# Four scheduling edits in an attention and Strassen-expert kernel: a pause in operand preparation, a load moved to SyncE, operands fetched two pieces ahead, and x sums queued together

## The chip, the cores and the metric

The kernel runs on one core of a Trainium2 chip. The metric is the device time of one execution in microseconds (us). Before the change three runs took 1164.88, 1165.45 and 1167.73 us; the median is 1165.45.

The core has five engines that this text names: PE (TensorE, matmuls; its weight loads are PEld), DVE (VectorE), ACT (ScalarE), POOL (GpSimd) and SP (SyncE, which here only issues DMAs). Each works through its own instructions in order and waits on semaphores for the others.

## What is computed

```python
# lightning attention, blocks of 64, (B, H, S, D) = (4, 8, 768, 64)
intra = einsum(q_b, k_b) * Dmask;  intra = intra @ v_b
inter = (q_b * lam_pow) @ kv_state;  out_b = intra + inter
kv_state = lam_block * kv_state + (k_b * rev_pow).T @ v_b
x = out.transpose(0, 2, 1, 3).reshape(3072, 512)
# four experts, F = 1024
p = probs / (probs.sum(-1) + 1e-9)
out = sum over e of p[:, e:e+1] * (relu(x @ w1[e]) @ w2[e])
```

All of it is in float32.

## The kernel before

**Groups and units.** The 3072 tokens are three groups of 1024. A unit is one expert on one group; there are twelve. While PE computes the second product (hidden times w2) of one unit, it computes the first product (x times w1) of the next one, interleaved: each unit has seven steps (`i`), one for each of Strassen's seven products, and each step eight slots (`x`) that alternate between second and first product (L1659 and on). Unit 0 begins at about 92 us. Before it lie the attention of group 0 and the first product of unit 0, written out as a list of calls (L1580 to 1590); the attention of the other groups is put into slots of later units.

**Plain and nested units.** Both products use Strassen's scheme. The first product (L1047) uses it twice, one level inside the other. The second product is plain, with one level, in the first five units (`second_product`, L1101), and nested from unit 5 on (`nested_product`, L1400; `NEST = 2 * E - 3`, L140). The first nested unit begins at about 600 us. A nested product needs gated hidden blocks (`gated`, L875: POOL multiplies by the gate, `m<-m,decay`), their sums (`outer_sums`, L888: ACT copies a block to a PSUM bank, `hp`, and DVE subtracts into `hT`; `inner_sums`, L918: POOL, `acc<-...`), and operands made of w2.

**Preparation.** The sums of the blocks of w1 and w2 that Strassen's products need are made by POOL ahead of time, stored in DRAM (`w1_ops`, `w2_ops`, `w2_sums`, all named w_ops or w_sums in the profile) and loaded back when they are due. These pieces of work are `chores` (for w2: `prepare_w2_ops`, L335; tiles `w2b`, `w2o`, `ops`). `pump` (L202), called after every slot, begins the next chore when a small model of POOL's and the DMA queues' load says so (`begins`, L208). `until` forces chores on when something is needed that isn't made yet. The stores go through a queue of their own and are issued by SP.

**Loads.** `send` (L109; the issue is L114) issues a DMA on SP unless told otherwise. `feed3` (L1139) loads an operand of a nested second product into tiles `w2t`, from a pool of six buffers (L75). Each of the seven pieces of a unit takes four tiles (`k` = 0 to 3; the last is half as large). Two are loaded at the begin of a step, and two behind slots 1 and 3 (L1681 and a few lines on); before the first nested unit two are loaded, so that the loads run two tiles ahead. `ws_in` are the operands of the first product, `xs` the x blocks and their sums. Results of group 1's plain unit are stored as `partial`, finished blocks as `parked`. The order in which SP issues all this is the order in which the program is written.

**Probabilities.** `load_probs` (L1570) loads the experts' probabilities (24 x 128 rows of 4 floats) into a part of the `decay` tile, issued by ACT. DVE makes the gates of it at about 72 us. A DMA's issue waits until the DMA before it that uses the same one of eight semaphores has landed; the semaphores are dealt out in turn over all issues of SP and ACT in the order of the built program.

**x sums.** The first product of unit 1 needs four subtractions (`x_steps`, L392) of each of seven x tiles. `own_x` (L1433) puts those of a tile into `own_sums`; the slots take them from there, one at a time, when DVE's modelled load allows it, and `first_product` (L1023) takes what is left when it needs them.

Of the kernel before, what the change touches and what calls it, by code (L numbers as in the profile page):

```python
# [21 lines left out]
def kernel(  # L22
# [30 lines left out]
    nc = tc.nc  # L53
# [4 lines left out]
    P = nc.NUM_PARTITIONS  # L58
# [42 lines left out]
    def packet(ap):  # L101
        n, step = 1, 1
        for stride, size in reversed(ap.ap[1:]):
            if stride != step or size == 1 and stride != 1:
                break
            n, step = n * size, step * size
        return n

    def send(out, in_, by=None):  # L109
        n = 4 * min(packet(out), packet(in_))  # L110
        moved[0] = max(moved[0], now[0]) + 4 * math.prod(out.shape) / n * (9 + n / 25) / 16 / 1714
        if by is None:
            asked[0] = max(asked[0], now[0]) + 0.27
        (by or nc.sync).dma_start(out=out, in_=in_)  # L114
# [13 lines left out]
    now, busy, free, filled, moved, asked, spare = [0], [0.0], [0.0], [0.0], [0.0], [0.0], []  # L128
# [11 lines left out]
    NEST = 2 * E - 3  # L140
# [46 lines left out]


    chores, queue, late, results, made = [], [], [], [], set()
    LEFT, packed = 1, []  # L190
    FULL = 4

    def store(f):
# [8 lines left out]
    def pump(pace=1.0, force=False):  # L202
        all_added(None if force else now[0])
        while results:
            results.pop(0)()
        while late and (force or late[0][0] <= now[0]):
            late.pop(0)[1]()
        begins = chores and (  # L208
            force or free[0] <= now[0] and max(moved[0], asked[0]) < now[0] + FULL
            and not (packed and busy[0] > now[0] + 1)  # L210
        )
        while queue and (force or queue[0][0] <= now[0] or begins and len(queue) > LEFT):
            queue.pop(0)[1]()
        if begins:
            begin = free[0] = max(free[0], now[0] - 1)
            was = max(busy[0], now[0])
            chores.pop(0)()
            free[0] = max(free[0], begin + max(pace * (busy[0] - was), (5 if len(chores) > 13 else 7) if spare else 1))
# [298 lines left out]
    for r in range(2):  # L517
        for ac in range(NHP):
            h = 4 * r + ac
            nc.vector.tensor_tensor_scan(  # L520
                out=s_decay[:, r, ac], data0=lam_bc[:, h:h + 1].to_broadcast([P, BL]), data1=blk_ident,
# [10 lines left out]
    for ac in range(NHP):  # L532
        nc.vector.tensor_tensor_scan(
            out=q_decay[:, ac], data0=lam_q[:, ac:ac + 1].to_broadcast([P, BL]), data1=zeros[:, 0:BL],
# [15 lines left out]
    probs = decay[:, 6, 0:96].rearrange("p (t e) -> p t e", e=E)  # L550
# [391 lines left out]
    SEQ = ("M1", "M5", "M6", "M2", "M7", "M3", "M4")  # L942
# [490 lines left out]
    def own_x(m, g=0, wait=0):  # L1433

        steps = to_do[m] = []

        def sub(f):
            def step():
                steps.pop()
                f()  # L1440
                if not steps:
                    made.add(("x", g, m))

            steps.append(step)

        for f in x_steps(g, m, nc.vector):
            sub(f)
        own_sums.extend(after(wait, f) for f in steps)
# [119 lines left out]
        chores.extend((*prepare_w2(0), *(raw[n] for n in ("A11", "A22", "A21"))))  # L1568

    def load_probs():  # L1570
        nc.scalar.dma_start(out=probs, in_=moe_domain_probs.rearrange("(t p) e -> p t e", p=P))

    def loads(*of):
        return lambda: [raw_w1(0, x) if isinstance(x, str) else load(x) for x in of]
# [84 lines left out]
    for at, (g, e) in enumerate(units):  # L1659
        if at == 0:  # L1660
            chores.extend(prepare_w2(2) + prepare_w1(3) + prepare_w2(3))
            chores.extend(prepare_w2_ops(2, False) + prepare_w1(0))
            for x in (3, 0):
                chores.extend(prepare_w2_ops(x, True))
        ahead = units[at + 1] if at + 1 < len(units) else None
        nested, nests = at >= NEST, ahead and at + 1 >= NEST
        if at == NEST:
            until(("w1", 0, "M4"))
            chores.extend(prepare_w2_ops(1, True))
            spare.append(True)  # L1670
        if at == NEST - 1:
            forget()
            packed.append(True)
        blocks, banks = {}, {}
        for i in range(7):
            if fill2:
                feed2(*fill2.pop(0))
            if not nested:
                later_operands(g, e, SEQ2[i])
            if nested or (nests and i == 6):  # L1680
                for _ in range(2 if ahead else 16 if i == 0 else 4 if i > 1 else 0):  # L1681
                    if fill3:
                        feed3(*fill3.pop(0))
            if nests and i == 2:
                nc.scalar.dma_start(
                    out=gate_bc, in_=gate_rows[ahead[0] - 1, :, ahead[1]].partition_broadcast(P),
                )
            if nested:
                pair = (at * 7 + i) % 2 if ahead else i % 3
                b = nested_product(at, SEQ3[i], (("q01", "q02"), ("q11", "q12"), ("g1", "g3"))[pair])  # L1690
                if i < 6 and (at, SEQ3[i + 1]) != PLAIN:
                    inner_sums(at, SEQ3[i + 1])
            else:
                b = second_product(g, e, SEQ2[i], banks)
            if nests and i == 6:
                inner_sums(at + 1, SEQ3[0], nested)
                if at + 1 == EARLY[0]:
                    inner_sums(*EARLY, True)
            a = []
            if ahead:  # L1700
                a = first_product(*ahead, SEQ[i], blocks, ("g1", "g3"))
            if nested and (at, SEQ3[i]) == END:
                b[6:6] = [lambda: (give("M4", 1, ("s0", "s1"), (1,)), turn_end(1, "q11"))]
                b[5:5] = [lambda: (give("M4", 0, ("s0", "s1"), (1,)), turn_end(0, "q12"))]
            if not ahead:
                order = [[], b[0:2], [], b[2:4], [], b[4:6], [], b[6:]]
            elif nested:
                order = [b[0:2], a[0:2], b[2:4], a[2:4], b[4:6], a[4:6], b[6:8], a[6:8]]
            else:
                order = [b[0:1], a[0:2], b[1:2], a[2:4], b[2:3], a[4:6], b[3:5], a[6:8]]  # L1710
            turned_back = list(after_last.get(SEQ3[i], ())) if nested and not ahead else []
            if at == 0 and i < 6:
                own_x(SEQ[i + 1])
            for x, part in enumerate(order):
                for f in part:
                    if f:
                        f()
                now[0] += 1
                if (at - 2 * E + 1, i, x) in first_steps:
                    first_steps.pop((at - 2 * E + 1, i, x))()  # L1720
                if joins:
                    joined()
                elif (ahead or x % 2 == 0 and x + i) and not (nests and i == 6 and x == 7):
                    if nested or nests:
                        rest()
                    else:
                        took = False
                        for of in (lately, background, own_sums):
                            if of and (not took or fits() or of is background and len(of) > 1):
                                take(of)  # L1730
                                took = True
                if nested or nests:
                    take(aside)
                    if own_sums and fits():
                        take(own_sums)
                if ending and fits():
                    end_first()
                if nested and ahead and x in (1, 3) and fill3:
                    feed3(*fill3.pop(0))
                if turned_back and x > 0:  # L1740
                    for y in turned_back.pop(0):
                        if SEQ3[i] == END[1]:
                            give(*y[:2], ("s0", "s1"), *y[2:])
                        else:
                            give_across(*y)
                if fill and at * 7 + i >= 6 and x in ((0, 1) if at * 7 + i < 13 else (1, 3, 5) if at * 7 + i == 13 else FEED[nested]):
                    feed(*fill.pop(0))
                while steps and (at * 7 + i) * 8 + x == steps[0][0]:
                    steps.pop(0)[1]()
                if at == 0 or x % 2:  # L1750
                    trickle(1, nc.scalar if at == 0 and x % 2 else None)
                for h in range(1, NG):
                    if x == 3 and 0 <= at * 7 + i - FILL[h] < 7:
                        x_fill(h, SEQ[at * 7 + i - FILL[h]])
                pump(PACE[g])
# [30 lines left out]
```

## Time and profile before

| | |
|---|---|
| median of three runs | 1165.45 us |
| the profiled execution | 1169.61 us |
| its span, first to last instruction | 1167.8 us |
| PE busy | 1148.6 us (98%) |
| PEld busy | 993.3 us (85%) |
| DVE busy | 824.5 us (71%) |
| POOL busy | 796.9 us (68%) |
| ACT busy | 317.1 us (27%) |
| DMA packets | 309258, 269.21 MB, mean 231 GB/s |
| mean granted TensorE clock | 0.995 |

Times in the profile are counted from the span's start. A timeline line gives start, duration, engine, source line, operation, what it writes and reads (`out<-in`), the number of merged instructions, and in brackets the idle time before it with what ended it. Lines of the waits give total, times and longest. L117 is the helper that issues every tensor_tensor, L114 the one that issues most DMAs, so those are told apart by their tiles. Names lose their numbers: `m` are all blocks of the hidden layer, `pg`, `pM`, `pq` and `q` are PSUM banks of the products. A float32 matmul is recorded as two instructions.

### The profile page before, as it was taken

Reading aid. Unit: us, or ns where it says so; the run is one execution under the profiler, and the core shown is the slowest. Engines: PE = TensorE matmul, PEld = TensorE weight load, DVE = VectorE, ACT = ScalarE, POOL = GpSimd, SP = SyncE. Lnnn points to the kernel's source line nnn. Section 1 sums busy time; section 2 is a strip of 40 time slices with the busy share of each in tenths; the row PEclk is TensorE's granted clock in tenths of the full one; section 3 lists DMA queues with packets and bytes.
Section 4 is the critical chain, followed back from the end, with each engine's and each line's share of the span. In section 5 each row is a group of like instructions: output and inputs, shape, how many; then the busy total and the mean of one; then the engine's idle time right before and its main releaser. Section 6 shows DMA issues by size and latency. Waiting matters only on the chain.

```text
span 1167.8 us, 21962 instructions
## 1 busy us (share of the span) xinstructions
PE 1148.6 (98%) x8011; PEld 993.3 (85%) x8011; DVE 824.5 (71%) x1516; ACT 317.1 (27%) x638; POOL 796.9 (68%) x752
## 2 busy tenths in 40 slices
PE   8899999999999999999999999999999999999998
PEld 7788888888888888888878888888888888888887
DVE  4485786578478857946765677998875677777785
ACT  4312122112201211221233342232243342341231
POOL 2836417746742984774796798896897793793894
PEclk9899999999999999999999999999999999999999
DMA  9894667999899999796867678966767866657542
GB/s 195 198 280 125 182 196 216 298 290 292 263 313 306 286 301 304 231 350 201 276 189 231 198 217 256 328 206 195 222 224 254 236 179 201 176 177 207 158 189 72
DMA packets 309258, 269.21 MB, mean 231 GB/s; under 512 B 141536, under 2 KB 244128, under 8 KB 309152
## 3 DMA queue, kind: packets, MB, share of 16 engines
q1 hardware_dynamic: 287744, 262.48, 73.6%
q10 hardware_dynamic: 21408, 5.33, 2.3%
q8 instruction: 64, 1.05, 0.4%
q14 instruction: 42, 0.34, 0.1%
HBM read 194.83 MB, written 77.10 MB: 233 GB/s over the span
## 4 chain that ended last, share of the span: by engine, by line
PE 85%; POOL 6%; DVE 4%; DMA 3%; issue 1%; SPq 1%; ACT 0%; ACTq 0%; POOLq 0%; DVEq 0%
PE pg L1047 35%; PE pq L1400 21%; PE q L1101 18%; POOL acc L117 3%; PE pM L1502 2%; DVE m L117 2%; PE pc L1502 2%; POOL m L117 2%; PE op L748 1%; PE sp L694 1%; DMA w2t<-w_ops 1%; PE op L766 1%; SPq L114 1%; PE sp L701 1%; DVE sums L117 1%
## 5 line engine op out<-in xcount | busy, mean ns | idle before, releaser
L1047 PE MATMUL pg<-xs,ws_in 128*128 128x256 f32 x1960 | 473.3, 381 | 4.9 <-DVE m L117 4.7
L1047 PEld LDWEIGHTS pg<-xs,ws_in 128*128 128x128 f32 x1960 | 368.5, 190 | 60.7 <-DVE m L117 10.7
L117 DVE TENSOR_TENSOR m<-pg,m 128x512 f32<-128x512 f32 x451 | 307.8, 688 | 122.4 <-PE pg L1047 105.4
L1101 PE MATMUL q<-w2t,m 128*128 128x256 f32 x1120 | 264.6, 379 | 0.0
L1101 PEld LDWEIGHTS q<-w2t,m 128*128 128x128 f32 x1120 | 212.7, 190 | 29.0
L117 POOL TENSOR_TENSOR m<-m,decay 128x512 f32<-128x512 f32 x112 | 143.4, 1299 | 83.6 <-ACT m L1059 75.5
L1400 PE MATMUL pq<-acc,w2t 128*128 128x256 f32 x688 | 170.5, 381 | 1.5 <-DMA w2t<-w_ops 1.4
L117 DVE TENSOR_TENSOR sums<-pq,sums 128x256 f32<-128x256 f32 x272 | 113.1, 421 | 71.9 <-PE pq L1400 64.4
L1400 PEld LDWEIGHTS pq<-acc,w2t 128*128 128x128 f32 x688 | 130.9, 191 | 20.8 <-issue 2.3
L1059 ACT ACTIVATE m<-m 128x512 f32<-128x512 f32 x132 | 83.1, 632 | 197.7 <-DVE m L117 191.4
L117 DVE TENSOR_TENSOR m<-m,m 128x512 f32<-128x512 f32 x112 | 97.1, 867 | 3.5 <-ACT m L1059 3.5
L1055 ACT COPY m<-pg 128x512 f32<-128x512 f32 x88 | 51.6, 587 | 147.1 <-PE pg L1047 137.3
L1119 DVE SCALAR_TENSOR_TENSOR acc<-q,gate,acc 128x256 f32<-128x256 f32 x108 | 51.9, 480 | 51.0 <-PE q L1101 50.5
L117 POOL TENSOR_TENSOR acc<-hT,hT 128x512 f32<-128x512 f32 x56 | 71.0, 1284 | 14.1 <-PE pq L1400 14.1
L117 POOL TENSOR_TENSOR acc<-hT,acc 128x512 f32<-128x512 f32 x56 | 71.4, 1275 | 6.4 <-PE pq L1400 1.8
L1400 PE MATMUL pq<-hT,w2t 128*128 128x256 f32 x288 | 74.0, 379 | 0.1
L979 ACT COPY up<-m 128x512 f32<-128x512 f32 x56 | 32.5, 590 | 127.5 <-DVE m L117 127.3
L117 POOL TENSOR_TENSOR w2o<-w2b 128x512 f32<-128x512 f32 x26 | 34.4, 1347 | 42.6 <-DMA w2b<-in_moe_w_dram 30.0
L1400 PEld LDWEIGHTS pq<-hT,w2t 128*128 128x128 f32 x288 | 54.6, 190 | 7.9 <-DVE sums L117 0.5
L899 ACT COPY hp<-m 128x512 f32<-128x512 f32 x84 | 48.5, 590 | 43.8 <-POOL m L117 22.2
L1400 PE MATMUL pq<-m,w2t 128*128 128x256 f32 x228 | 59.4, 384 | 0.1
L117 POOL TENSOR_TENSOR xs<-xs 128x256 f32<-128x256 f32 x28 | 23.8, 849 | 42.5 <-DMA xs<-x_blocks 40.9
(140 smaller groups left out, 1365.3 us busy)
## 6 DMA issues: line engine op xcount, KB each, us to landing
w2t<-w_ops SPq DMA_DIRECT2D x129, 256.0 KB, 4.0
ws_in<-w_ops SPq DMA_DIRECT2D x40, 512.0 KB, 5.2
ws_in<-w_ops SPq DMA_DIRECT2D x60, 256.0 KB, 3.6
ws_in<-w_ops SPq DMA_DIRECT2D x40, 384.0 KB, 3.7
w2b<-in_moe_w_dram SPq DMA_DIRECT2D x56, 256.0 KB, 5.1
w_ops<-ops SPq DMA_DIRECT2D x28, 512.0 KB, 4.8
w2t<-w_sums SPq DMA_DIRECT2D x40, 256.0 KB, 4.5
w_sums<-w2o SPq DMA_DIRECT2D x16, 512.0 KB, 5.0
```

What stands on the lines that cost most here:

```text
L114: (by or nc.sync).dma_start(out=out, in_=in_)
L117: eng.tensor_tensor(out=o, in0=a, in1=b, op=op)
L694: nc.tensor.matmul(out=sp[r][half[x], ac * BL:(ac + 1) * BL], lhsT=hc(kT)[half[r], ac, blk[x]], rhs=hc(qT)[half[r], ac, blk[x]], start=(ac ...
L899: nc.scalar.copy(out=there[x][:], in_=blk[at][:])
L979: nc.scalar.copy(out=there[at][:], in_=a[at][:])
L1047: nc.tensor.matmul(out=p[:, j * 256:(j + 1) * 256], lhsT=ws[i][:, j * P:(j + 1) * P], rhs=xs[i], start=(fresh and j == 0), stop=True, skip ...
L1055: nc.scalar.copy(out=new[at][:], in_=p[:])
L1059: nc.scalar.activation(out=new[at][:], in_=new[at][:], func=AF.Relu)
L1101: nc.tensor.matmul(out=p[:, s * DH:(s + 1) * DH], lhsT=h[A_OF[m]][:, c * 256 + s * P:c * 256 + (s + 1) * P], rhs=fed2[g, e, m][uu][:, c], ...
L1119: nc.vector.scalar_tensor_tensor(out=o, in0=x, scalar=w, in1=o, op0=ALU.mult, op1=ALU.add)
L1400: nc.tensor.matmul(out=p[:, 0:256], lhsT=fed3[e, m, x // 2][:, x % 2, c * P:(c + 1) * P], rhs=b[B_OF[i]][:, c * 256:(c + 1) * 256], start= ...
L1502: nc.tensor.matmul(out=p[:, s * 256:(s + 1) * 256], lhsT=a[c][:, f:f + P], rhs=b[:, c, j * 256:(j + 1) * 256], start=(s == 0 and c == 0 an ...
```

## The change

There are four edits.

1. A flag `resting` is set in the last two steps of the last plain unit and in the first step of the first nested one; while it is set, no chore begins (unless it is forced).
2. `load_probs` issues its DMA through `send`, on SP.
3. At the last step before the first nested unit four operand tiles are loaded instead of two, so that the nested units' loads run four tiles, one whole piece more, ahead.
4. The x sums of all six remaining tiles are queued in the first step of unit 0, instead of one tile's in each step.

```diff
-    LEFT, packed = 1, []
+    LEFT, packed, resting = 1, [], [False]
...
-            force or free[0] <= now[0] and max(moved[0], asked[0]) < now[0] + FULL
+            force or free[0] <= now[0] and max(moved[0], asked[0]) < now[0] + FULL and not resting[0]
             and not (packed and busy[0] > now[0] + 1)
...
     def load_probs():
-        nc.scalar.dma_start(out=probs, in_=moe_domain_probs.rearrange("(t p) e -> p t e", p=P))
+        send(out=probs, in_=moe_domain_probs.rearrange("(t p) e -> p t e", p=P))
...
             if nested or (nests and i == 6):
-                for _ in range(2 if ahead else 16 if i == 0 else 4 if i > 1 else 0):
+                for _ in range(4 if not nested else 2 if ahead else 16 if i == 0 else 4 if i > 1 else 0):
                     if fill3:
                         feed3(*fill3.pop(0))
...
-            if at == 0 and i < 6:
-                own_x(SEQ[i + 1])
+            if at == i == 0:
+                for m in SEQ[1:]:
+                    own_x(m)
+            resting[0] = at == NEST - 1 and i >= 5 or at == NEST and i == 0
```

`nests` is true while the next unit is nested, `ahead` is the next unit, `at` the number of the unit whose second product runs. The instructions of PE and ACT keep their order (ACT loses the one DMA issue); those of POOL, DVE and SP change places as the edits say.

## The prediction

> **What bounds the kernel now.** I read the page's busy line and clock digits first, then TensorE's waits, then the timeline at each wait. The page:
>
> ```profile
> span 1167.8 us, 21962 instructions
> PE 1148.6 (98%) x8011; PEld 993.3 (85%) x8011; DVE 824.5 (71%) x1516; ACT 317.1 (27%) x638; POOL 796.9 (68%) x752
> ...
> PEclk9899999999999999999999999999999999999999
> ```
>
> TensorE is the bound and 98% busy, and the change leaves its instructions and their order as they were. So the time can only move in the 19 us in which PE idles, and where the granted clock drops. TensorE's waits (us in total, times, longest):
>
> ```profile
> PE pg L1047 <- DVE m L117: 5.7, 8, 2.5
> PE op L766 <- issue: 2.7, 2, 2.2
> PE pM L1502 <- ACT m L1512: 2.0, 1, 2.0
> PE pq L1400 <- DMA w2t<-w_ops: 1.4, 1, 1.4
> ```
>
> The second line lies in the first 45 us, before anything that changes. Of the others the longest are few, at 50, 184, 600 and 894 us, and each edit meets one. The table by stretches (PE, PEld, DVE, ACT, POOL busy; then granted clock, DMA share, GB/s) shows what a long wait also costs:
>
> ```profile
> 51.20:58.00 6.80, 5.91 (x74) 4.54 (x73) 5.14 (x11) 1.71 (x6) 5.86 (x6) 0.50 0.81 179
> 600.70:604.10 3.40, 3.40 (x10) 2.69 (x9) 3.15 (x6) 2.23 (x5) 3.40 (x3) 0.50 0.65 210
> ```
>
> After the two longest waits (starts 2.2 us late at 50.4, 2.6 us late at 599.8) the clock is 0.50: a 128x256 matmul starts every 0.43 us there, against 0.216 us (1.73 us for 8) elsewhere. After delays of 1.2 to 1.6 us (184, 392, 894) it stayed at 1.00.
>
> The Trainium skill, TensorE: Matmul & The Clock Gate, "Part 1: The HAM clock gate (the "warmup" mystery)", says the clock halves after an idle window of about 3.4 us. By it neither wait would cost clock, and the sum below would lose 3 to 4 us. The granted clock of these rows disagrees, so I count it.
>
> **Edit 1, probabilities issued by SyncE.** ACT and PE around 50 us:
>
> ```profile
> 42.56 0.59 ACT L673 COPY kT<-kp 128x512 f32<-128x512 f32 x1
> 49.29 0.38 ACTq L1571 DMA_DIRECT2D decay<-in_moe_domain_probs_dram  x1
> 49.77 0.59 ACT L1512 COPY m<-pM 128x512 f32<-128x512 f32 x1 [6.61 <-DMA w2b<-in_moe_w_dram]
> ```
>
> ```profile
> 50.40 3.05 PE L1502 MATMUL pM<-xs,w1b 128*128 128x256 f32 x8 [2.02 <-ACT m L1512]
> 54.35 1.13 PE L748 MATMUL op<-qs,kv 64*64 64x64 f32 x32 [0.89 <-DVE kv L117]
> ```
>
> ACT stands from 43.15 to 49.29 because its own DMA issue waits until a w2b load that SP issued at 45.97 has landed (49.27): both update the same DMA semaphore. Behind the issue stand the copy that frees PE's bank and the copies that DVE needs. In the built order of the changed kernel the load stands on SP right after the last v load (SP at 40.1) and waits for a load issued long before, so ACT is free at 43.15. What it cost: PE could have gone on at 48.22; up to 56.26 (8.04 us) it did 8 matmuls (1.73) and two groups of small ones (1.09, as at 37.84 to 38.93), so 5.2 us were lost. The next 32 matmuls ran from 56.26 to 64.12 instead of 6.91 us: 0.95 more. Together 6.1 us.
>
> Next late is DVE's kv. PE started L748 4.58 us after ACT's copy at 49.77; the copy can now start at 46.2, when its matmuls end, so L748 at 50.8. PE is there at 49.96 and waits about 0.8 us: too short for the clock, by the cases above. **Gain 5.3 us**, bounds 2.2 (only the first wait goes, and the clock still drops) and 6.1.
>
> SP pays one issue, 0.4 us, and has 3,072 pieces of 16 bytes ahead of the w2b loads. In the trace this DMA took 4.3 us from issue to landing. What is behind feeds POOL's sums for w2; the tiles made from them landed at 84.2 and PE reads them at 104.95, so up to 15 us are covered and I take nothing. The Trainium skill, DMA: Bandwidth & Descriptors, "Queues, rings and completion order", speaks against the edit: descriptors of one issuing engine are consumed in ring order, while rows of two engines are served in turn. By it w2b is late by up to those 4.3 us; the 15 us still cover it.
>
> PE earlier by 5 us meets operands at 58 to 120 us. The sums for the next w1 (POOL, ops at 102.3 to 105.3, needed from 107.4) hang on a w2b load at 97.78, which waits on ACT's DMAs, which follow PE: they move along. Everything else there has over 10 us. Nothing charged.
>
> **Edit 2, x sums queued at once.** All 24 subtractions (DVE, 128x256, 0.42 us) now enter at the first step of unit 0, which takes 13 us, instead of one tile's four per step. The built order has 8 more of them in its first two steps (3.4 us); DVE idles some 13 us between 92 and 120, so they are covered. In the last step one is left where four stood; there four took 3.55 us (178.71 to 182.26, POOL sharing), so DVE is 2.6 us earlier. PE's late start at 184.14 (1.24 us, on DVE's m) goes. The next wait, 188.90, is on POOL's kn at 188.85, whose chain starts at 177.5 on something else; without three DVE sums beside it POOL loses less (its sums there took 0.9 to 1.06 us against 0.73), about 1.0 us. **Gain 1.0 us**, bounds 0 (POOL's kn takes all back) and 1.9.
>
> **Edit 3, no preparation around the begin of the nested units.** Around 600 us:
>
> ```profile
> 578.55 2.50 POOL L117 TENSOR_TENSOR w2o<-w2b,w2o 128x512 f32<-128x512 f32 x2
> ...
> 581.02 9.20 POOL L117 TENSOR_TENSOR m<-m,decay 128x512 f32<-128x512 f32 x6
> ...
> 596.64 0.59 ACT L899 COPY hp<-m 128x512 f32<-128x512 f32 x1 [9.63 <-POOL m L117]
> ...
> 599.83 1.23 PE L1047 MATMUL pg<-xs,ws_in 128*128 128x256 f32 x4 [2.45 <-DVE m L117]
> ```
>
> POOL runs without a gap from 575.6 to 599.1, and ACT (hp), DVE (hT, then m) and PE stand behind it one after the other. In the built order the two w2o sums go from before the six gate products to some 80 matmuls later; the four ops before them stay. So the chain is 2.47 us earlier (581.02 less 578.55), if its inputs are there: the relu results come at 575.9 to 584.1, and the store that frees an acc tile landed at 590.55 against 591.6. PE's delay was 2.61; 0.15 is left, and the half clock goes (8 matmuls in 3.35 instead of 1.73: 1.6 us). **Gain 4.1 us**, bounds 0 and 4.3.
>
> The moved work comes back. Later pieces of preparation slip by 6 to 21 us of program, and are caught up in unit 6, where one step (about 734 to 746) now holds 16.9 us of POOL work instead of 13.4, at 1.27 and 0.73 us each, with 12.1 us of PE. POOL was up to 10 us behind PE there (each sum against the matmuls beside it in the built order), and DVE let PE wait 0.4 us. But at 838 to 841 POOL was 13 us behind and PE did not wait. I charge 0.5 us, bounds 0 and 5.3 (3.5 us of POOL on PE's path, plus 1.8 of half clock). The nearest deadline, expert 0's second piece, is stored 7.8 us of program before its first load instead of 17.7; a store lands in about 5 us and the load is due 12 us before use. No charge.
>
> **Edit 4, w2 operands two pieces ahead.** Two more tiles are loaded before the first nested unit, so that every load is half a piece earlier. The late one was this:
>
> ```profile
> 883.11 0.37 SPq L114 DMA_DIRECT2D parked<-sums  x1
> 883.87 0.37 SPq L114 DMA_DIRECT2D w_ops<-w2o  x1
> ...
> 887.39 1.42 SPq L114 DMA_DIRECT2D w2t<-w_ops  x3
> ```
>
> Six stores stand ahead of the third w2t, which landed at 893.63 for a PE that was ready at 892.2. In the built order that load stands right after parked, 4.5 us earlier. **Gain 1.5 us**, bounds 0 and 1.55. The price: with six buffers, the last loads of a piece now wait for PE to release the piece being computed, and behind them on SP stand ws_in, the w_ops stores and the result stores. ws_in waits for PE at about the same point already; its landing takes 3.6 to 5.2 us, its use is about 12 us later. No charge.
>
> **Sum.** 5.3 + 1.0 + 4.1 - 0.5 + 1.5 = 11.4 us. The profiled execution took 1169.6 us (span 1167.8), so 1158.2 of its kind; the median of the runs is 1165.45, so 1154.1. The profiled one is 4.2 us above that median, so some of these waits may be shorter in unprofiled runs.
>
> **Rivals.**
> - **Half of it** (0.20): ACT's place is taken by DVE's kv with the clock still dropping (gain 2.2), or POOL's delayed pieces cost a wait with half clock in unit 6 (-5.3). For: DVE idles 7 us behind ACT, and POOL is the second most loaded. Against: the 4.58 us chain, and 13 us of lag borne at 840. About 1165.45 less 6 = 1159.5.
> - **It does not do what it says** (0.06): the waits are of the profiled execution (it is the one 4.2 us longer), or what is freed is taken by the next wait (kn at 188.9, m at 602). About 1164.
> - **Slower** (0.06): SP in step with PE. The third w2t of each step waits for PE; if a w_ops store behind it waits for POOL longer than the 7 us that ws_in has (12.1 less 5.2), PE loses over 2 us and then half clock, 3.9 us in each of six units: 1154 + 23 = 1177. Against: SP waited for POOL's ops 9.0 us in all over 13 times, 3.3 at most.
>
> **How the numbers follow.** The forecast has 0.68. A measurement of this kernel tells 0.3% (3.5 us) from no change. Half of it and the forecast are faster by more than that but for a little: faster 0.87, same 0.07, slower 0.06. The range goes from 1150.5 (all upper bounds, 13.9 us, give 1151.6; other small DVE waits at 737 to 775 may go) to 1161.5, which takes in half of it.
>
> **What would show it.** After: no ACT idle over 3 us at 43 to 50 and no half clock before 60; a wait of about 1 us for kv; nothing at 184; the wait near 590 under 0.5 us and clock 1.00; w2t no longer a releaser near 882; PE's idle time 8 to 10 us instead of 19. I am wrong if PE waits over 2 us anywhere after 60 us, most likely for DVE m near 730 to 760, or for a DMA behind SP.

## The result, and the profile after

The changed kernel took 1161.41 us (median of 7 runs, 1159.49 to 1163.88). Seven runs of the kernel before, on the same chip, had a median of 1165.45 us. The ratio is 0.9965, with a 95% interval of 0.9951 to 0.9979: 4 us faster (2.4 to 5.7), where 11.4 were forecast. Measured again beside the experiments, it was 0.9957 (0.9941 to 0.9973).

The two profiled executions are further apart than the medians: 1169.61 and 1160.99 us, 8.6 us. The page of the kernel after:

```profile
span 1159.2 us, 22045 instructions
PE 1143.5 (99%) x8011; PEld 991.6 (86%) x8011; DVE 836.6 (72%) x1516; ACT 317.0 (27%) x638; POOL 796.3 (69%) x752
...
PEclk9999999999999999999999999999999999999999
```

PE idles 15.7 us (1159.2 less 1143.5) instead of 19.2, where 8 to 10 were forecast. The clock digits have no 8 any more. TensorE's waits (us in total, times, longest):

```profile
PE pM L1502 <- DVE m L117: 2.5, 1, 2.5
PE pg L1047 <- DVE m L117: 2.3, 7, 0.8
PE op L766 <- issue: 2.1, 1, 2.1
PE kp L664 <- DMA kn<-in_k_dram: 1.5, 3, 0.9
PE sp L701 <- POOL kn L117: 1.3, 1, 1.3
```

Against the list of before: ACT and the w2t loads are gone as releasers, and DVE's 5.7 us before the `pg` products are 2.3. The first line is new, and so is the size of the last (0.4 before). These two are where time was given back. The fourth is new against before too, but it lies before 45 us, and profiles of kernels with the load on ACT have it as well (0.2 to 0.8 us). The brackets of a timeline are idle time; where this text calls PE late by some us, it counts from when PE could have gone on, which is 0.15 to 0.2 us more. The new wait, in PE's timeline:

```profile
72.84 3.62 PE L1502 MATMUL pM<-xs,w1o 128*128 128x256 f32 x16
78.92 3.72 PE L1502 MATMUL pM<-xs,w1o 128*128 128x256 f32 x16 [2.46 <-DVE m L117]
```

What DVE did meanwhile, in the same kernel:

```profile
67.45 0.25 DVE L561 TENSOR_REDUCE decay<-decay 128x24 f32<-128x96 f32 x1
...
68.58 2.36 DVE L571 COPY gate<-decay 128x4 f32<-128x4 f32 x9
...
75.19 2.47 DVE L117 TENSOR_TENSOR m<-pc,m 128x512 f32<-128x512 f32 x4
77.59 0.68 DVE L117 TENSOR_TENSOR m<-m,m 128x512 f32<-128x512 f32 x1
78.19 1.28 DVE L117 TENSOR_TENSOR m<-pM,m 128x512 f32<-128x512 f32 x2
```

From 67.45 to 75.19 DVE computes the experts' gates: four operations and 32 copies of 4 elements per partition. Only then come the sums that empty the banks in which PE wants to go on. The same place in the profile of before, DVE and PE:

```profile
72.43 0.25 DVE L561 TENSOR_REDUCE decay<-decay 128x24 f32<-128x96 f32 x1
...
74.34 0.74 DVE L571 COPY gate<-decay 128x4 f32<-128x4 f32 x9
...
76.62 2.48 DVE L117 TENSOR_TENSOR m<-pc,m 128x512 f32<-128x512 f32 x4
```

```profile
77.93 7.16 PE L1502 MATMUL pM<-xs,w1o 128*128 128x256 f32 x32
```

PE did not wait there. The gates began equally far ahead of PE's `pM` products in both (5.5 us before, 5.4 after); DVE and PE had both come earlier. What differs is the length of the stretch: 4.2 us before and 7.7 us after; groups of nine equal copies took 0.74 and 2.36 us. And there was no room for more: in the profile of before the DVE sum that frees the bank ended at 81.32 us, and the second half of the `pM` matmuls began at 81.38.

POOL's sums for w1 ran from 68.58 to 74.33 beside the slow copies; before, they had ended at 73.64, ahead of the first copy. In all the profiles of this study there are 344 gate copies. Of the 260 without a POOL operation beside them none held DVE for over 0.1 us; of the 84 with one beside them 26 held it for 0.6 us or more. So the slow copies all lie beside POOL's work, but no run moves that work alone.

### The profile page after: what moved, and what is told of

The parts are those of the page before. It is cut to its first block, busy times and chain, and to the rows that moved or that the text cites. A ratio compares the mean times of both kernels' runs of the same rounds, so it can differ in the third digit from the quotient of the medians.

```text
span 1159.2 us, 22045 instructions
## 1 busy us (share of the span) xinstructions
PE 1143.5 (99%) x8011; PEld 991.6 (86%) x8011; DVE 836.6 (72%) x1516; ACT 317.0 (27%) x638; POOL 796.3 (69%) x752
## 4 chain that ended last, share of the span: by engine, by line
PE 88%; DVE 7%; DMA 2%; POOL 1%; issue 1%; SPq 0%; ACT 0%; ACTq 0%; DVEq 0%; POOLq 0%
PE pg L1047 38%; PE pq L1400 22%; PE q L1101 19%; DVE m L117 3%; PE pM L1502 2%; DVE sums L117 1%; PE sp L694 1%; PE op L748 1%; DVE xs L117 1%; PE op L766 1%; PE sp L701 1%; DMA kn<-in_k_dram 1%; PE kp L664 1%; PE pc L1502 1%; PE qp L664 1%
## 5 line engine op out<-in xcount | busy, mean ns | idle before, releaser
L117 DVE TENSOR_TENSOR m<-m,m 128x512 f32<-128x512 f32 x112 | 100.5, 897 | 3.5 <-ACT m L1059 3.5
```

The lines of the kernel that those rows point to most:

```text
L117: eng.tensor_tensor(out=o, in0=a, in1=b, op=op)
```

## The experiments

**Theory A**: the forecast's sum was measured on an untypical execution, whose half clock is not in the usual run. **Theory B**: the terms were right, and the changed kernel gives part back in new waits, above all at the gates. The edits are numbered as in the prediction, not as in the list of the change: 1 is the load of the probabilities on SP, 2 the x sums, 3 the pause in preparation (`resting`), 4 the w2 operands. Each kernel was run beside the kernel before, in turn on the same chip (another one for each of the four sets), with the ratio over all their runs. Gains in us are (1 - ratio) times the median of before in that set (1168.27, 1166.89, 1167.58 and 1167.04).

**The kernel before, again** (no edit).

> The kernel before, unchanged, for the clock of each of its runs and a second profile. Theory A (the sum was measured on an untypical execution: the half clock after the waits near 51 and 600 us, 10.2 us of it or 5.1 us lost, is not in the usual run): mean granted clock 0.998 or more in the runs near 1165, and 0.995 only in those near 1167.5; a second profile shows at least one of the two half-clock stretches absent, and the terms of the edits 1 and 3 shrink by 2 to 3 us each. Theory B (the terms were right, and the changed kernel gives part of them back in new waits, above all the 2.6 us for VectorE near 79 us): the clock is near 0.995 in nearly all runs and the second profile shows both stretches.

Ratio 1.0006 (0.9992 to 1.002). Its profiled execution had a clock of 0.999. ACT and the clock in it:

```profile
47.85 0.38 ACTq L1571 DMA_DIRECT2D decay<-in_moe_domain_probs_dram  x1
48.32 0.58 ACT L1512 COPY m<-pM 128x512 f32<-128x512 f32 x1 [2.79 <-PE op L766]
```

```profile
51.20:58.00 6.80, 6.80 (x91) 5.79 (x90) 4.49 (x11) 1.85 (x6) 6.05 (x5) 1.00 0.61 141
597.50:600.90 3.40, 3.23 (x8) 2.60 (x9) 3.21 (x7) 2.40 (x5) 2.54 (x3) 0.50 0.60 161
```

The issue of the probabilities came 1.4 us earlier than in the first profile. No wait of PE for ACT followed, and no half clock at 51 to 58; the one near 600 was there. So edit 1's stall is not in every run. Seven profiles of kernels that load the probabilities on ACT were taken in all: in four PE starts late for ACT at 50 to 52 us (2.2, 2.0, 1.9 and 1.5 us), and in one alone the half clock follows. The clock of 101 runs of the kernel before averages 0.9978, and 6 of them are as low as the profiled 0.995. In time the profiled execution is less unusual: the median of the 101 is 1167.56 us, and 14 of them took as long as its 1169.61 or longer. Theory A holds for this term.

**Edit 1 alone.**

```diff
-        nc.scalar.dma_start(out=probs, in_=moe_domain_probs.rearrange("(t p) e -> p t e", p=P))
+        send(out=probs, in_=moe_domain_probs.rearrange("(t p) e -> p t e", p=P))
```

> Only the first edit: the probabilities loaded by SyncE. Theory A: 1 to 3 us faster than before (about 1163), since the half clock behind its wait is seldom there. Theory B: the prediction's 5.3 us less the new wait at the gates, if this edit alone already brings it (about 1162.5), or the full 5.3 (1160) if it does not; the profile shows PE's wait for VectorE near 79 us in the first case.

Ratio 0.9998 (0.9986 to 1.0011): 0.2 us, interval -1.3 to 1.6. PE's timeline has the gates' wait with this edit alone:

```profile
78.38 3.72 PE L1502 MATMUL pM<-xs,w1o 128*128 128x256 f32 x16 [1.31 <-DVE m L117]
```

Less than either theory gave to it, though the interval takes in the lower end of A's 1 to 3. Part of what the edit gains before 60 us is lost again by 80; the kernels with fewer copies, below, show it.

**Edit 3 alone** (the flag `resting`, as in the change).

```diff
+            resting[0] = at == NEST - 1 and i >= 5 or at == NEST and i == 0
```

> Only the third edit: no preparation around the begin of the nested units. Theory A: 1.5 to 2.5 us faster (about 1163.5), the wait near 600 us without the half clock behind it being some 2 us. Theory B: the full 3.6 us of the prediction (about 1162).

Ratio 0.9968 (0.9955 to 0.9982): 3.7 us (2.1 to 5.3). The place in PE's timeline:

```profile
595.77 1.13 PE L1047 MATMUL pg<-xs,ws_in 128*128 128x256 f32 x4
...
598.84 1.35 PE L1047 MATMUL pg<-xs,ws_in 128*128 128x256 f32 x5 [0.21 <-DVE m L117]
```

The first line has no bracket: PE came 0.25 us late there and 0.38 late at the second, where it had come 2.6 late. The time is theory B's value (3.6); of A's 1.5 to 2.5 the interval holds the upper end. Of the seven profiles of kernels without this edit, the wait near 600 is 2.5 us in five and 1.3 in two, and in four the half clock follows: most of it is there in the usual run.

**Edit 4 alone.**

```diff
-                for _ in range(2 if ahead else 16 if i == 0 else 4 if i > 1 else 0):
+                for _ in range(4 if not nested else 2 if ahead else 16 if i == 0 else 4 if i > 1 else 0):
```

> Only the fourth edit: w2 operands asked for two pieces ahead. Both theories: up to 1.5 us faster (1164 to 1165.5), with no wait of PE for an operand near 893 us in its profile. If the time does not move although the wait is gone, the wait was either absent from the usual run or has gone to another place in the last units.

Ratio 0.9986 (0.9976 to 0.9996): 1.6 us (0.5 to 2.8). Between 884 and 896 us PE's timeline has no wait, and the time moved by the wait's size. (Two tiles are half a piece: the loads now run one piece ahead, where they ran half a piece.)

**Edit 2 alone.**

```diff
-            if at == 0 and i < 6:
-                own_x(SEQ[i + 1])
+            if at == i == 0:
+                for m in SEQ[1:]:
+                    own_x(m)
```

> Only the second edit: the x sums of unit 0 queued at once. The prediction's term: 1.0 us faster than before, bounds 0 and 1.9, with the late start of 1.2 us near 182 us gone. If GpSimd's kn, some 5 us later, takes all of it back: no difference, and a late start of 1.5 us or more at kn in its place.

Ratio 0.9998 (0.9985 to 1.001): 0.2 us, interval -1.2 to 1.8. The wait for DVE is gone, the one for `kn` is longer (1.53 us late instead of 0.65):

```profile
186.14 0.69 PE L701 MATMUL sp<-vn,kn 64*64 64x64 f32 x32 [1.32 <-POOL kn L117]
```

**The changed kernel, again** (no edit).

> The changed kernel as it is, again, beside the others of this set, for its clocks and a second profile. Both theories: 0.3 to 0.4% under before, as measured, and PE's late start near 79 us again, behind VectorE's gates.

Ratio 0.9957 (0.9941 to 0.9973). The late start at the gates was 0.98 us in this execution (2.62 in the first).

**The changed kernel without edit 1.**

```diff
-        send(out=probs, in_=moe_domain_probs.rearrange("(t p) e -> p t e", p=P))
+        nc.scalar.dma_start(out=probs, in_=moe_domain_probs.rearrange("(t p) e -> p t e", p=P))
```

> The changed kernel without the first edit (probabilities again loaded by ScalarE's queue); the other three stay. If the first edit is worth nothing in a usual run, because its gain is absent or given back at the gates: the same time as the changed kernel within 1 us, and no late start near 79 us in the profile. If it is worth the forecast 5.3: 5 us slower than the changed kernel, that is no faster than before.

Ratio 0.9963 (0.995 to 0.9975), as the changed kernel within 0.7 us. In its profile the wait for ACT is back (2.0 us at 52.31) and there is none at the gates. As the change stands, its first edit brings nothing that can be measured.

**The changed kernel with few gate copies.** One copy takes all tokens of one expert group that lie in a regular pattern: 128x16 elements, 8 copies in place of 32, the same values. (This edit moves the later line numbers by 7.)

```diff
-        for n in range(NG * CPG):
-            t = token(*where_of(n)) // P
-            if n < LAST * CPG:
-                nc.vector.tensor_copy(out=gate[:, n], in_=gates_of[:, t])
...
+        by_x = gates_of.rearrange("p (b c) e -> p c b e", b=B)
+        by_pair = gates_of.rearrange("p (x h c) e -> p h x c e", x=B // 2, h=2)
+        for c in range(2):
+            nc.vector.tensor_copy(out=gate[:, 4 * c:4 * c + 4], in_=by_x[:, c])
...
+                            in_=by_pair[:, h, :, 2 * g:2 * g + 2].rearrange("p x c e -> p x (c e)"),
```

> The changed kernel with the gates of the experts copied by 8 instructions with more elements each, instead of 32 copies of 4 elements; same values. In the changed kernel's trace these copies held VectorE from 68.6 to 75.2 us, right ahead of the four sums for which PE started 2.6 us late at 78.9. Theory B (what the first edit gains is given back at the gates): VectorE comes 3 to 5 us earlier to those sums, PE's late start goes, and the kernel is 2 to 2.6 us faster than the changed kernel. Rival A (the first edit had hardly anything to gain in a usual run): the stall may go, but the time is within 1 us of the changed kernel, as another wait before 130 us takes its place.

Ratio 0.9932 (0.992 to 0.9945), 2.9 us below the changed kernel of this set (roughly 0.5 to 5.3, estimated from the two intervals). DVE and PE at the place:

```profile
68.91 0.24 DVE L561 TENSOR_REDUCE decay<-decay 128x24 f32<-128x96 f32 x1
...
72.46 2.71 DVE L117 TENSOR_TENSOR m<-pc,m 128x512 f32<-128x512 f32 x4
...
76.21 0.69 DVE L117 TENSOR_TENSOR m<-pM,m 128x512 f32<-128x512 f32 x1 [0.27 <-PE pM L1509]
```

```profile
74.28 7.07 PE L1509 MATMUL pM<-xs,w1o 128*128 128x256 f32 x32
```

The gates take 3.6 us. DVE now waits for PE (the bracket), and PE runs its 32 matmuls through, where they were cut in two. But a shorter gate stretch could be worth this by itself, so it was tried on the kernel before, without and with edit 1.

**The kernel before with few gate copies** (the edit above, on before).

> The kernel before with the 8 gate copies in place of 32, a control: is the shorter stretch of VectorE worth something by itself? In the profile of before TensorE comes late to this place and does not wait for the gates. If few gates only give back what the first edit lost there: no difference to before (within 1 us). If they are worth their 3 us anyway: 2 to 3 us faster than before, and the changed kernel's gain from them says nothing of the first edit.

Ratio 0.9996 (0.9982 to 1.0011): 0.5 us, interval -1.3 to 2.1.

**The kernel before with edit 1 and few gate copies** (both edits above).

> The kernel before with the first edit and the 8 gate copies, nothing else. If the first edit's gain was lost at the gates: 2 to 3 us faster than before, where the first edit alone was 0.2 us faster. If the first edit has nothing to give: the same as the control with the 8 copies alone.

Ratio 0.9966 (0.9953 to 0.998): 4.0 us (2.3 to 5.5). Edit 1 alone gives 0.2, the copies alone 0.5, both together 4.0. By itself neither brings anything that can be measured; together they bring 3.3 us more than their sum (roughly 0.5 to 6, estimated from the three intervals, of two sets). Theory B holds here, with its size uncertain.

**A tile of k decayed early: the wrong one.** POOL's product of a k tile with the decay was moved ahead of the transposes, into a tile of its own, for the first k tile of the second token group (`n == CPG`), on the changed kernel with few copies.

```diff
-        kd = kn if n >= CPG else small("kd")[:].rearrange("p (h d) -> p h d", d=D)
+        kd = kn if n > CPG else small("kd")[:].rearrange("p (h d) -> p h d", d=D)
...
+            if n == CPG:
+                put(s - 4, lambda n=n: decayed(n))
```

> The changed kernel with the 8 gate copies, and the decay of the first k tile of the second token group moved ahead of the transposes into a tile of its own. The second edit alone brought nothing, since PE's late start for VectorE near 181 us went and the one for GpSimd's kn 5 us later grew from 0.65 to 1.5 us. If that is where it went: 1 to 1.5 us faster than the changed kernel with the 8 copies, and no late start over 0.5 us near 185. If the state that GpSimd passes on just ahead of kn (kv, 0.6 us) is the later of the two: 0.3 to 0.6 us at most.

Ratio 0.9954 (0.9938 to 0.997): nothing gained. The kernel with few copies alone measured 0.9932 in the set before and 0.9945 in the next, so sets differ by 1.5 us or more, and the 2.9 us above is no exact size. PE still starts 1.53 us late at 185.58, for `kn`. In POOL's timeline the new `kd` stands at 114; the tile that PE waits for at 185 is the third of its group. The run tells nothing of the second edit.

**The same with the third tile**, beside its partner without it and one without edit 2.

```diff
+        kd = kn if n >= CPG and n != CPG + 2 else small("kd")[:].rearrange("p (h d) -> p h d", d=D)
...
+            if n == CPG + 2:
+                put(s - 4, lambda n=n: decayed(n))
```

> The changed kernel with the 8 gate copies, again, beside the next two: 0.6 to 0.7% under before, and PE's late start of 1.5 us for GpSimd's kn near 185 us.

> The same with the decay of the third k tile of the second token group (the one of which PE waits near 185 us; the run before had moved the first one's) moved ahead of the transposes, into a tile of its own. If GpSimd's kn is where the second edit's gain went: no late start over 0.3 us near 185 and 1.2 to 1.5 us faster than with the 8 copies alone. If VectorE's m is as late as kn, or the moved time comes back further on: the same time within 0.7 us.

> The same without the second edit. If kn hid the second edit's gain: PE starts 1.2 us late for VectorE's m near 181 us, and the kernel is about 1 us slower than the run just above. If the second edit has nothing to give even so: the same time within 0.5 us.

The ratios are 0.9945 (0.9928 to 0.9961) with few copies, 0.9935 (0.9922 to 0.9947) with the early tile too, and 0.9943 (0.993 to 0.9956) without edit 2: 1.2 us gained, then 0.9 lost, both inside the intervals. The profiles tell them apart better. With the early tile PE has no wait left at this place:

```profile
181.90 0.69 PE L701 MATMUL sp<-qT,kT 64*64 64x64 f32 x32
182.42 0.65 PE L708 MATMUL sp<-vn,kd 64*64 64x64 f32 x32
```

Without edit 2 the old wait for DVE is back, 5 us ahead of it:

```profile
180.94 1.10 PE L1056 MATMUL pg<-xs,ops 128*128 128x256 f32 x4 [0.97 <-DVE m L117]
```

Both go the way that "kn hid it" says, about by its size; the waits show it, the times alone do not. The kernel with few copies and the early tile, 1158.93 us (median of 6 runs, 0.65% under before), has the lowest median of the study, though it is not told apart from the one with few copies alone (1159.64 and 1159.65 in its two sets).

## Why the prediction was right about four stalls and wrong about what the first is worth

All four stalls that it named went: ACT never idles over 2.5 us between 43 and 50 in the profile after, the wait for DVE at 184 is gone (the one for kn is longer instead), the starts near 594 and 597 are 0.25 and 0.38 us late, and w2t is no releaser any more. The wait of about 1 us for kv, expected behind edit 1, did not come. Term by term, each edit alone:

| edit | forecast, us | measured alone (interval) |
|---|---|---|
| 1, probabilities on SP | 5.3 | 0.2 (-1.3 to 1.6); 4.0 (2.3 to 5.5) with few gate copies |
| 2, x sums at once | 1.0 | 0.2 (-1.2 to 1.8) |
| 3, pause in preparation | 4.1 - 0.5 | 3.7 (2.1 to 5.3) |
| 4, w2 operands ahead | 1.5 | 1.6 (0.5 to 2.8) |

Alone they add up to 5.8 us (before rounding); the whole change measured 4.1 and 5.0. Edits 3 and 4 were right in size, closer than their intervals can tell. The charge of 0.5 us for the late preparation was right too: PE's late start at 731 us in unit 6 is 0.93 us, where it was 0.40 at 738. The rival of a slower kernel (SP in step with PE) left no trace: no DMA behind SP made PE wait after 60 us.

**The step that failed is edit 1's "Everything else there has over 10 us. Nothing charged."** It looked at loads and at POOL's operands between 58 and 120 us, and not at DVE, whose 36 small operations for the gates lie at 67 to 77 with no room behind them (81.32 against 81.38, above). Three things meet there. PE and DVE come 2 to 3 us earlier with the edit. SP's later issues come later: the first of the w1b loads behind the probabilities is issued at 61.3 us on the mean of the seven profiles with the load on ACT, and at 63.8 in the nine with it on SP; POOL's first sum of them starts at 66.0 and at 68.7. The prediction took nothing for what stands behind the load, because w2's tiles had 15 us. So POOL's sums, which began 5 us ahead of the gates, now begin as the gates do. And the 32 copies beside them take long: the gates took 4.2 to 5.1 us in the six profiles without the edit, and 5.6, 5.6 and 7.7 in the three with it.

PE's instructions are the same in all these kernels up to here, so its lead can be read off at each (mean start in the seven profiles with the load on ACT, less the mean of the others):

| PE at (us in the profile of before) | lead, edit 1 and 32 copies (3 profiles) | lead, edit 1 and few copies (6 profiles) |
|---|---|---|
| 54, L748 group | 2.9 | 2.7 |
| 78, begin of the `pM` products | 3.0 | 2.1 |
| 82, their second half | 1.3 | 2.2 |
| 131 | 1.3 | 2.1 |

The gates take 1.7 us of 3.0 with 32 copies, and nothing with few. (Three of the six with few copies wait 0.6 to 0.7 us for DVE's `xs` near 60; the profiles do not say why.) The prediction had said that it would be wrong if PE waited over 2 us after 60 us. It did, but at 79 for the gates, not "near 730 to 760".

**The second failure is the clock in edit 1's term.** The terms came from one execution, in which 10.2 us ran at half clock and 5.1 us were lost. Of edit 1's 5.3 us some 3.1 are this (2.1 of the 5.2 up to 56.26 are neither of its two waits, and all of the 0.95 behind), of edit 3's 4.1 us 1.6: together 4.7, more than the "3 to 4 us" that the text itself said. The half clock behind edit 1's wait is in one of seven profiles, the one near 600 in four of seven. The usual run of before loses 0.0022 x 1166 = 2.6 us to the clock (101 runs), that of after 0.0013 x 1161 = 1.5 us (15 runs): about 1 us to be saved, not 5. The pair of profiles makes it visible: 8.6 us between them, less the 4 us of clock that the usual runs don't have, is 4.6, and 4.1 and 5.0 were measured. The text had said that "some of these waits may be shorter in unprofiled runs" and gave it no number. So edit 1 had some 3.0 us to give, not 5.3, and 1.3 of them are left behind the gates; the timed 0.2 and, with few copies, 4.0 lie 1 us below and 2 us above the leads of 1.3 and 2.1, and this stays open.

**Edit 2's 1.0 us was its upper half.** The bound "0 (POOL's kn takes all back)" was the case: kn's late start grew by 0.9 us, as the DVE wait of 1.24 went. POOL's work from 177.5 to the end of kn took 11.3 us in the profile of before and 10.9 with edit 2 alone: 0.4 us faster for want of DVE's sums beside it, not 1.0.

Of the rivals, "half of it" (1159.5 us) was the nearest in number, by mechanisms that did not occur. The one that says "the waits are of the profiled execution" named the second reason, and went too far with 1164 us: the stall near 600 and the one near 894 are in the usual run too. How much of the missing 7 us the gates took and how much the clock is not settled closer than 1.5 us: the late start at the gates varies from 1.0 to 2.6 us between three profiles, and the timed gain from few copies was 2.9 us in one set.

## What to carry to other kernels

When an edit brings the bound engine earlier by some us, walk every other engine's program through that stretch: which engines come along, which do not or come later, what lies side by side for the first time, and how much room each sum that the bound engine needs has left. A run of many tiny instructions is easily overlooked, because no group of them is large. Take a sum from a profiled execution only after asking how far that execution is from the median, and take out of the terms what the usual run does not have, clock first. Where an edit brings nothing, try it together with the removal of the next wait before dropping it: here two edits that measured 0.2 and 0.5 us measured 4.0 together.

## What the runs showed of the hardware

The granted clock moves on a grid. In the first profile of before it is 1.00 first at 6.81 us and falls to 0.50 at 51.18, 44.37 us later; the next stretches last 6.83, 542.72 and 3.41 us. These are 13, 2, 159 and 1 times 3.4133 us. In all 16 profiles the changes of clock fit such a grid, which starts where TensorE first got the full clock.

What decides in these profiles is how much of one window of the grid TensorE idles, not the length of a wait. Fifteen times in these profiles (apart from the end of the kernel, and the second of the two windows at 51 us) a window was followed by half clock; TensorE had idled 1.85 to 2.45 us in it. In windows with up to 1.63 us nothing followed, and no window lies between. Nine of the fifteen lie at 11 to 17 us, around a wait of 2.2 us or so that no edit touches; this alone makes runs of one kernel differ by the 1.7 us that a window at half clock costs. The same wait of 2.5 us for DVE cost half clock in the kernel before, where it lay in one window (597.38 to 599.83, in the window from 597.31 to 600.73), and none with edit 2 alone, where it was cut 1.24 to 1.28:

```profile
596.74 1.13 PE L1047 MATMUL pg<-xs,ws_in 128*128 128x256 f32 x4 [2.53 <-DVE m L117]
```

```profile
597.00:600.40 3.40, 3.19 (x15) 2.48 (x15) 3.21 (x7) 2.56 (x6) 2.98 (x3) 1.00 0.56 165
```

The new wait of 2.5 us at 79 in the changed kernel was cut too, 1.63 to 0.83, and cost no clock. So whether a wait of 2 to 3 us costs another 1.7 us is a matter of where a run's grid lies, and belongs into a sum as a chance.

The Trainium skill, TensorE: Matmul & The Clock Gate, "Part 1: The HAM clock gate (the "warmup" mystery)", says that the window is free-running and 3413 ns long; the grid agrees with that. It gives an idle window as what leads to half rate; here 1.85 us of idle time in the 3.41, 54%, was enough, and 1.63 us, 48%, was not.
